# Experts' rows turned by a partition move and VectorE's block transpose in place of TensorE's transpose

## The chip, the cores and the metric

The kernel runs on one core of a Trainium2 chip. The metric is device time in microseconds (us) of one execution; lower is better. Engines: TensorE (PE; PEld is its weight load), VectorE (DVE), ScalarE (ACT), GpSimd (POOL), and SyncE (SP), which here only issues transfers. ACT and POOL have a queue for transfers too.

## The reference

Sliding-window attention (8 x 8 heads, 576 positions, head size 64, window 64) gives x, 4608 tokens of 512. A gate sends each token to one of 8 experts; a token keeps its predecessor's expert where a local gate is at least 0.5.

```python
logits = np.einsum('bsd,de->bse', x, w_gate)
local_gate = 1.0 / (1.0 + np.exp(-np.einsum('bsd,de->bse', x, w_local).squeeze(-1)))
...
            if s == 0 or local_gate[b, s] < 0.5:
                e = fresh_e
            else:
                e = prev_e if prev_e >= 0 else fresh_e
...
            h = np.maximum(x[b, s] @ w1[e], 0.0)
            out[b, s] = p[e] * (h @ w2[e])
```

w1 is 512 x 1024 and w2 1024 x 512 per expert, all in float32.

## The kernel before, in words

The attention comes first and writes its rows to the DRAM tensor `xs`; a router builds tables of row numbers, so that each *job* is a group of tokens of one expert: big (two tiles of 128 rows), small (one tile), half (64 rows) or quarter (32 rows). `Experts.run` writes out the order of the jobs by hand. Numbered from 0 it is: three big jobs from the first part of the tokens (0 to 2), then big 3, big 4, small 5, big 6, quarter 7, big 8, small 9, big 10, big 11, small 12, big 13, quarter 14, big 15, small 16, big 17, big 18, half 19, big 20, big 21, big 22, half 23.

For a job, `rows` lets POOL gather its rows from `xs` into a tile `xg` [128, 528], a token to a partition; `weights` lets SP load w1 and w2 (2 MB each) into a ring of four buffers. So the weights of job k+2 take the buffers that job k frees: w1 when its first product is done, w2 near the end of its second. Both are asked for at the start of iteration k, for job k+2.

`turn` puts features on partitions: four TensorE transposes per tile into PSUM (`tp`, L1196) and a copy to `xt` (L1197, on DVE from job 4 on). An iteration of a big job k is: `hidden(k)`, seven products of Strassen's scheme of 16 matmuls each (`product`, L1268) with `keep` copies on ACT (L1274) that read PSUM tiles which a later product adds into; `turn(k+1)`; `result(k)`, seven products of 8 matmuls (L1318), whose outputs ACT (L1323, L1349) and DVE (L1327) scale, and POOL scatters (L1394). DVE makes the sums that Strassen's scheme needs of the inputs (`xs`), the weights (`ws`) and the hidden values (`hs`) (L1220, L1231). Small jobs take plain matmuls (L1414, L1455; ReLU on ACT at L1425 and on DVE at L1423), halves L1414 and L1442.

From job 2 on the order on PE, SP, DVE and ACT is as written in the code; each engine runs its instructions in that order. Transfers of SP and ACT count, in turn, on one of eight semaphores, DMAHW0 to DMAHW7, and a transfer is issued only when the one before it on the same semaphore has landed.

Of the kernel before, what the change touches and what calls it, by code (L numbers as in the profile page):

```python
# [8 lines left out]
F32 = mybir.dt.float32  # L9
I32 = mybir.dt.int32  # L10
U32 = mybir.dt.uint32
BF16 = mybir.dt.bfloat16
# [7 lines left out]
P = 128  # L20
# [62 lines left out]
@with_exitstack  # L83
def kernel(
    ctx: ExitStack,
    tc: tile.TileContext,
    q: bass.AP,
    k: bass.AP,
    v: bass.AP,
    kq: bass.AP,  # L90
    v3: bass.AP,
    v4: bass.AP,
    vt: bass.AP,
    vh: bass.AP,
    wg: bass.AP,
    wg2: bass.AP,
    w1: bass.AP,
    w2: bass.AP,
    out: bass.AP,
):  # L100
    nc = tc.nc
    const = ctx.enter_context(tc.tile_pool(name="const", bufs=1))
    dram = ctx.enter_context(tc.tile_pool(name="dram", bufs=1, space=DRAM))


    xs = dram.tile([N + 2, PITCH], F32, name="xs")
    lt = const.tile([P, C, E + 1], F32, name="lt")
    tabs = dict(idx=const.tile([P, NS], U32, name="idx"), ej=const.tile([1, NBLK + 1], I32, name="ej"),
                idxh=const.tile([P, E], U32, name="idxh"), idxq=const.tile([P, E], U32, name="idxq"),
                idx1=const.tile([P, FIRST], U32, name="idx1"), ej1=const.tile([1, FB], I32, name="ej1"),  # L110
                gx=const.tile([P, NS], U32, name="gx"), gx1=const.tile([P, FIRST], U32, name="gx1"))
    ident = const.tile([P, P], F32, name="ident")
    make_identity(nc, ident)
    wg2s = const.tile([P, HP, GW], F32, name="wg2s")
    nc.gpsimd.dma_start(out=wg2s, in_=wg2)
    wgs = const.tile([P, DK, GW], F32, name="wgs")
    nc.gpsimd.dma_start(out=wgs, in_=wg)
    ok = const.tile([P, 1], F32, name="ok")
    bad, rare = const.tile([1, 1], I32, name="bad"), const.tile([1, 1], I32, name="rare")

    moe = xs, w1, w2, out, tabs, lt, ident
    with ExitStack() as fast:
        ring = fast.enter_context(tc.tile_pool(name="ring", bufs=4))
        rt = Router(fast, tc, lt, xs, tabs, ident)
        ex = Experts(fast, tc, ring, *moe)
        zeros, n = ex.xp.tile([P, PITCH], F32, name="xg"), (ZR - T1) // HF
        nc.vector.memset(zeros[:HF], 0.0)
        for i in (ZR, N + 1):
            nc.gpsimd.dma_start(out=xs[i:i + 1, :], in_=zeros[:1])
        nc.gpsimd.dma_start(out=xs[T1:ZR, D:].rearrange("(c p) o -> p c o", p=HF),  # L130
                            in_=zeros[:HF, :n * (PITCH - D)].rearrange("p (c o) -> p c o", c=n))
        attention(tc, ring, kq, v3, v4, vt, vh, xs, lt, ok, wgs, wg2s, ident, rt, ex)
        ex.run(fast, rt, lambda ps: flag(nc, ps, ok, bad, tabs["ej"][:, NBLK:], rare, ident))
    if_rare = nc.values_load(rare[0:1, 0:1], min_val=0, max_val=1,  # L134
                             skip_runtime_bounds_check_because="the larger of two comparisons")
    with tc.If(if_rare > 0):
        if_bad = nc.values_load(bad[0:1, 0:1], min_val=0, max_val=1,
                                skip_runtime_bounds_check_because="the result of a comparison")
        with tc.If(if_bad > 0):
            careful(tc, q, k, v, xs, lt, wgs, ident)  # L140
            with ExitStack() as slow:
                ring = slow.enter_context(tc.tile_pool(name="ring2", bufs=4))
                rt = Router(slow, tc, lt, xs, tabs, ident)
                rt.prepare()
                ex = Experts(slow, tc, ring, *moe)
                with tc.tile_pool(name="rt_ps1", bufs=1, space=PSUM) as ps:
                    for _ in rt.first(lambda: ps.tile([P, SC], F32, name="a")):
                        pass
                ex.begin()
                ex.run(slow, rt)  # L150
        if_more = nc.values_load(tabs["ej"][0:1, NBLK:], min_val=0, max_val=1,
                                 skip_runtime_bounds_check_because="the larger of two comparisons")
        with tc.If(if_more > 0), ExitStack() as slow:
            ring = slow.enter_context(tc.tile_pool(name="ring3", bufs=4))
            Experts(slow, tc, ring, *moe).more(slow)
# [12 lines left out]
def attention(ctx, tc, ring, kq, v3, v4, vt, vh, xs, lt, ok, wg, wg2, ident, rt, ex):  # L168
# [68 lines left out]
    def until(i, x):  # L237

        nc.sync.dma_start(out=late[:, i:i + 1], in_=x)
# [231 lines left out]
    for i, (sc, hp) in enumerate(units):  # L471
# [51 lines left out]
        if hp == 2 and sc + 2 in GATED:  # L523
            load(sc + 2, ["turned"])
        if (sc, hp) == (NSC - 3, 3):
            ex.jobs = [ex.weights({}, -1, ("w1",), lambda: until(2, allr[:1, sc, hp, 0, :1]))]
            if side == ():
                ex.rows(ex.jobs[0], -1)
        step(not (hp == 2 and sc + 1 in GATED))
# [601 lines left out]
class Experts:  # L1131
# [7 lines left out]

    def fetch(self, n):  # L1140

        return self.weights(self.rows({}, n), n)

    def rows(self, st, n):
        tabs = self.tabs
        if n < 0:
            idx, gx, rows = tabs["idx1"], tabs["gx1"], ZR + 1
            slots = range(-2 - 2 * n, -2 * n)
        else:
            idx, gx, rows = tabs["idx"], tabs["gx"], N + 2  # L1150
            slots = range(2 * n, 2 * n + 2) if n < NB else range(SM0 + n - NB, SM0 + n - NB + 1)
            if n >= KINDS[2]:
                slots = range(HF0 + n - KINDS[2], HF0 + n - KINDS[2] + 1)
        st.update(x=[], slots=slots, idx=idx, rows=P, big=len(slots) == 2, fast1=len(slots) == 2 and n not in PLAIN1,
                  fast2=len(slots) == 2 and n not in PLAIN2)
        if n >= KINDS[2]:
            st.update(quarter=n - KINDS[2], rows=QR)
        elif n >= KINDS[1]:
            st.update(half=n - KINDS[1], rows=HF)
        for s in slots:  # L1160
            x = (self.xp if n == -1 else self.xq).tile([P, PITCH], F32, name="xg")
            asked = self.nc.gpsimd.indirect_dma_start(  # L1162
                out=x, out_offset=None, in_=self.xs[:rows, :],
                in_offset=bass.IndirectOffsetOnAxis(ap=gx[:, s:s + 1], axis=0))
            st["x"].append(x)
            st["asked"] = asked
        st["pw"] = [x[:, D:D + 1] for x in st["x"]]
        return st

    def weights(self, st, n, names=("w1", "w2"), behind=lambda: None):  # L1170
        ej, at = (self.tabs["ej1"], -1 - n) if n < 0 else (self.tabs["ej"], n)
        e = self.nc.values_load(ej[0:1, at:at + 1], engines=[ET.SP], min_val=0, max_val=E - 1,
                                skip_runtime_bounds_check_because="a count of experts, at most E - 1")
        behind()
        for name, w, a, b in (("w1", self.w1, DK, F), ("w2", self.w2, FK, D)):
            if name not in names:
                continue
            t = self.ring.tile([P, a * b], F32, name="w")
            src = w[bass.ds(e, 1)].rearrange("o p x -> (o p) x")
            m = a * b // (PARTS if n < 0 else 1)  # L1180
            for c in range(0, a * b, m):
                self.nc.sync.dma_start(out=t[:, c:c + m], in_=src[:, c:c + m])
            st[name] = t.rearrange("p (a b) -> p a b", a=a)
        return st
# [4 lines left out]
    def turn(self, st, quiet, later=False):  # L1189
        nc, n = self.nc, st["rows"]  # L1190
        a = slice(HF, HF + n) if "quarter" in st else slice(n)
        st["xt"] = xt = self.xtp.tile([P, DK, BIG], F32, name="xt")
        for i, x in enumerate(st["x"]):
            tp = self.ps_t.tile([P, DK, P], F32, name="tp")
            for kk in range(DK):
                nc.tensor.transpose(tp[:, kk, :n], x[a, kk * P:(kk + 1) * P], self.ident[a, a])  # L1196
            (nc.scalar.copy if quiet else nc.vector.tensor_copy)(xt[:, :, i * P:i * P + n], tp[:, :, :n])  # L1197
# [276 lines left out]
    def run(self, ctx, rt, last=None):  # L1474
# [3 lines left out]
        ps_r = ctx.enter_context(tc.tile_pool(name="ex_ps_r", bufs=1, space=PSUM))  # L1478
        ctx.enter_context(tc.manual_schedule(engines={ET.PE, ET.SP}))
        rt.rows_of(ctx, tc, "rt_oh2", 3)  # L1480
        jobs = self.jobs

        def psum():
# [35 lines left out]
        for i, n in enumerate(order):  # L1519
            quiet = i < FB  # L1520
            if i == FB - 1:
# [2 lines left out]
                mark = last(self.ps_y.tile([P, D], F32, name="yp")) if last else None  # L1524

                ctx.enter_context(tc.manual_schedule(engines={ET.PE, ET.SP, ET.DVE, ET.Activation}))
                st = self.rows({}, order[FB])
                with tc.issue_after(st["asked"].ins):
                    jobs[i - 1].pop("later")()
                jobs.append(self.weights(st, order[FB]))  # L1530
                if jobs[i]["fast1"]:
                    self.prepare(jobs[i])
            if i + 2 > FB and i + 2 < len(order):
                jobs.append(self.fetch(order[i + 2]))
            if n >= KINDS[2]:
                continue
            if i == 1:
# [81 lines left out]
```

## Time and profile before

| | us |
|---|---|
| median of 3 runs | 644.74 (644.02 to 646.02) |
| the profiled execution | 642.1 |
| its span, first to last instruction | 640.0 |
| TensorE busy in the span | 615.6 |
| DVE, ACT, POOL busy | 402.3, 200.6, 133.1 |
| hardware DMA queue of SP | 135.54 MB, 58.4% of 16 engines' span |

The attention takes the first fifth of the span; the products of the experts' jobs follow up to 625. Busy times of a group are a union, so that matmuls that overlap in the pipeline count once. A row of the timeline gives start, duration, engine, line, operation, output and input, and how many instructions it merges. "DMA to landing" is the time from a transfer's issue to its landing.

### The profile page before, as it was taken

Reading aid. Unit: us, or ns where it says so; the run is one execution under the profiler, and the core shown is the slowest. Engines: PE = TensorE matmul, PEld = TensorE weight load, DVE = VectorE, ACT = ScalarE, POOL = GpSimd, SP = SyncE. Lnnn points to the kernel's source line nnn. Section 1 sums busy time; section 2 is a strip of 40 time slices with the busy share of each in tenths; the row PEclk is TensorE's granted clock in tenths of the full one; section 3 lists DMA queues with packets and bytes.
Section 4 is the critical chain, followed back from the end, with each engine's and each line's share of the span. In section 5 each row is a group of like instructions: output and inputs, shape, how many; then the busy total and the mean of one; then the engine's idle time right before and its main releaser. Section 6 shows DMA issues by size and latency. Waiting matters only on the chain. (4 is left out here: it accounts for less than half of the span.)

```text
span 640.0 us, 14994 instructions
## 1 busy us (share of the span) xinstructions
PE 615.6 (96%) x6367; PEld 544.2 (85%) x6367; DVE 402.3 (63%) x752; ACT 200.6 (31%) x368; POOL 133.1 (21%) x132
## 2 busy tenths in 40 slices
PE   8889998899999999999999999999999999999995
PEld 7777777788889999978997999887997998899994
DVE  6676588879968775273654683362917752886730
ACT  3766765612572122113120312021211221213120
POOL 5422112430103202120302120211312022111101
PEclk9999998999999999999999999999999999999998
DMA  9999996969757645786958665769768556956501
GB/s 338 416 418 406 385 366 241 348 236 337 237 171 246 244 166 198 242 316 236 387 189 291 218 234 212 259 235 367 263 228 324 185 199 232 379 167 225 209 17 38
DMA packets 29318, 166.43 MB, mean 260 GB/s; under 512 B 8451, under 2 KB 9497, under 8 KB 20026
## 3 DMA queue, kind: packets, MB, share of 16 engines
q1 hardware_dynamic: 20394, 135.54, 58.4%
q0 software_dynamic: 8848, 29.85, 12.2%
q8 instruction: 52, 0.85, 0.5%
q14 instruction: 24, 0.20, 0.1%
HBM read 146.18 MB, written 19.59 MB: 259 GB/s over the span
## 5 line engine op out<-in xcount | busy, mean ns | idle before, releaser
L1394 POOL DMA_INDIRECT out_dram<-y,idx x36 | 41.1, 1141 | 339.1 <-DVE y L1327 196.5
L1318 PE MATMUL hp<-ws,hs 128*128 128x256 f32 x384 | 88.7, 380 | 0.0
L1318 PEld LDWEIGHTS hp<-ws,hs 128*128 128x128 f32 x384 | 72.6, 190 | 10.5 <-issue 0.8
L1268 PE MATMUL hp<-xs,ws 128*128 128x128 f32 x672 | 79.6, 275 | 0.0
L1268 PEld LDWEIGHTS hp<-xs,ws 128*128 128x128 f32 x672 | 77.3, 192 | 0.0
L1327 DVE SCALAR_TENSOR_TENSOR y<-hp,xg,kept 128x256 f32<-128x256 f32 x48 | 22.6, 482 | 74.2 <-issue 47.0
L1414 PE MATMUL hp<-xt,w 128*64 128x64 f32 (+2 forms) x640 | 66.2, 276 | 0.0
L1414 PEld LDWEIGHTS hp<-xt,w 128*128 128x128 f32 (+1 forms) x640 | 60.8, 170 | 4.1 <-issue 0.7
L1318 PE MATMUL hp<-w,h 128*128 128x256 f32 x256 | 61.1, 382 | 0.0
L1162 POOL DMA_INDIRECT xg<-xs,gx x40 | 50.3, 1258 | 45.6 <-issue 37.4
L1279 DVE TENSOR_TENSOR h<-hp,keep 128x512 f32<-128x512 f32 x42 | 28.6, 690 | 48.1 <-PE hp L1268 48.0
L1268 PEld LDWEIGHTS hp<-xt,w 128*128 128x128 f32 x448 | 53.2, 192 | 2.7 <-issue 1.3
L1268 PE MATMUL hp<-xt,w 128*128 128x128 f32 x448 | 54.7, 275 | 0.0
L1318 PEld LDWEIGHTS hp<-w,h 128*128 128x128 f32 x256 | 47.2, 190 | 6.3 <-issue 0.4
L431 PE MATMUL xo<-vb,p 128*64 128x74 f32 (+1 forms) x576 | 44.5, 230 | 7.0 <-issue 2.9
L416 ACT ACTIVATE p<-sp 128x512 f32<-128x512 f32 x72 | 39.2, 595 | 38.0 <-PE sp L385 35.9
L385 PEld LDWEIGHTS sp<-w 64*64 64x64 f32 x1296 | 38.7, 138 | 12.1 <-issue 8.5
L421 DVE TENSOR_TENSOR p<-p,mask 128x1024 f32<-128x1024 f32 x29 | 36.1, 1245 | 19.5 <-ACT p L416 19.3
L431 PEld LDWEIGHTS xo<-vb,p 128*64 128x64 f32 x576 | 38.9, 138 | 9.9 <-issue 4.4
L385 PE MATMUL sp<-w 64*64 64x128 f32 (+1 forms) x1296 | 43.8, 270 | 2.6 <-issue 1.5
L431 PE MATMUL xo<-va,p 128*64 128x74 f32 (+1 forms) x576 | 44.5, 230 | 1.2 <-issue 1.2
L1280 ACT ACTIVATE h<-h 128x512 f32<-128x512 f32 x42 | 26.3, 630 | 59.1 <-DVE h L1279 59.1
(280 smaller groups left out, 955.0 us busy)
## 6 DMA issues: line engine op xcount, KB each, us to landing
w<-in_w_dram SPq DMA_DIRECT2D x42, 2048.0 KB, 9.2
w<-in_kq_dram SPq DMA_DIRECT2D x17, 1024.0 KB, 8.7
w<-in_w_dram SPq DMA_DIRECT2D x24, 512.0 KB, 9.3
xs<-x POOLq DMA_DIRECT2D x9, 1024.0 KB, 9.5
va<-in_v_dram SPq DMA_DIRECT2D x5, 1184.0 KB, 8.9
vtt<-in_vt_dram SPq DMA_DIRECT2D x5, 1024.0 KB, 7.2
va<-in_v_dram SPq DMA_DIRECT2D x3, 1040.0 KB, 12.2
va<-in_v_dram SPq DMA_DIRECT2D x2, 520.0 KB, 6.8
```

Source lines behind the costliest of these rows:

```text
L385: nc.tensor.matmul(sp[j][c * WIN:(c + 1) * WIN, a:b], lhsT=kt[h, hp, block * WIN:(block + 1) * WIN], rhs=qt[h, hp, a:b], start=not biased, ...
L416: nc.scalar.activation(p[:, j], sp[j], Act.Exp, scale=DH ** -0.5)
L421: masked.append(nc.vector.tensor_tensor(p, p, m.to_broadcast([P, 2, SC]), op=Alu.mult))
L431: nc.tensor.matmul(xo[par * WIN:(par + 1) * WIN, j, s * VW:s * VW + n], lhsT=p[:, j, b * WIN:(b + 1) * WIN], rhs=w[:, s, 2 * hp + j, :n], ...
L1162: asked = self.nc.gpsimd.indirect_dma_start(out=x, out_offset=None, in_=self.xs[:rows, :], in_offset=bass.IndirectOffsetOnAxis(ap=gx[:, s: ...
L1268: nc.tensor.matmul(out[:, m, :], lhsT=a[:, kk, m * P:(m + 1) * P], rhs=b[:, kk, :], start=start and m + kk == 0, stop=stop and (m, kk) == ...
L1279: nc.vector.tensor_tensor(o, x, y, op=add)
L1280: nc.scalar.activation(o, x if y is None else o, Act.Relu)
L1318: nc.tensor.matmul(out, lhsT=a[:, m, :], rhs=b[:, m, :], start=start and m == 0, stop=stop and m == FK // 2 - 1, skip_group_check=True)
L1327: nc.vector.scalar_tensor_tensor(y[i][:, j * w:(j + 1) * w], x, pw[i], y2, Alu.mult, Alu.add)
L1394: self.nc.gpsimd.indirect_dma_start(out=self.out[:, :], out_offset=bass.IndirectOffsetOnAxis(ap=st["idx"][:, s:s + 1], axis=0), in_=y, in_ ...
L1414: nc.tensor.matmul(hp[a, i, :], lhsT=st["w1"][:, kk, m * P:(m + 1) * P][:, a], rhs=st["xt"][:, kk, :n], start=(kk == 0), stop=(kk == DK - 1))
```

## The change

For the jobs of whole tiles from job 4 on (12 big, 4 small) TensorE's transposes and the copy from PSUM go. In their place `spread` (new) lets ACT issue four transfers per tile, each moving 128 features of 128 tokens from `xg` to a group of 32 partitions of a tile `rowh`: token 4t+m lands on partition t of the group, in slot m, in pieces of 512 bytes. `turn` then has DVE transpose blocks of 32x32 of that tile straight into `xt`. Features so lie on other partitions than before, and the load takes w1 from a host array `w1t` with its rows in the matching order. `rowh` tiles come from a pool of three that the router used for its tables.

```diff
@@ Experts.rows
+        st["plain"] = plain or n < 0 or st["rows"] < P
@@ Experts, new
+    def spread(self, st):
+
+        if st["plain"]:
+            return
+        st["sh"] = []
+        for x in st["x"]:
+            sh = self.shp.tile([P, PIECE, P], BF16, name="rowh")[:, :2 * DK].rearrange("p m t -> p (m t)")
+            sh = sh.bitcast(F32).rearrange("p (m t) -> p m t", m=4)
+            for a in range(4):
+                self.nc.scalar.dma_start(out=sh[a * QR:(a + 1) * QR].rearrange("t m d -> t (m d)"),
+                                         in_=x[:, a * P:(a + 1) * P])
+            st["sh"].append(sh)
@@ Experts.weights
-        for name, w, a, b in (("w1", self.w1, DK, F), ("w2", self.w2, FK, D)):
+        for name, w, a, b in (("w1", self.w1[not st["plain"]], DK, F), ("w2", self.w2, FK, D)):
@@ Experts.turn
         for i, x in enumerate(st["x"]):
+            if not st["plain"]:
+                nc.vector.transpose(xt[:, :, i * P:(i + 1) * P].rearrange("p j (t m) -> p m j t", m=4),
+                                    st["sh"][i].rearrange("p m (j d) -> p m j d", j=DK))
+                continue
             tp = self.ps_t.tile([P, DK, P], F32, name="tp")
@@ Experts.run
+        self.shp = rt.oh_p
...
+            if i >= FB and i + 1 < len(order) and not jobs[i + 1]["shared"]:
+                self.spread(jobs[i + 1])
             if i + 2 > FB and i + 2 < len(order):
-                jobs.append(self.fetch(order[i + 2]))
+                st = self.rows({}, order[i + 2])
+                st["shared"] = order[i + 1] >= KINDS[2]
+                if st["shared"]:
+                    self.spread(st)
+                jobs.append(self.weights(st, order[i + 2]))
@@ kernel (host)
+        "w1t": i["moe_w1"].reshape(E, 4, DK, QR, F).transpose(0, 1, 3, 2, 4).reshape(E, P, DK * F),
```

So the moves for job k+1 are issued at the start of iteration k. Where job k+1 is a quarter, it has none, and those of job k+2 are issued there instead.

On ACT, at the end of job 2's `result` and the start of job 3's `hidden`, with what each row waits for, there stood before:

```order
153 L1323 ACTIVATE kept_3167<-hp,xg 128x256 [waits PE_49]
154 L1349 ACTIVATE y<-hp,xg 128x256 [waits DMASW1_49,PE_49,Activation_49]
155 L1274 COPY keep_3221<-hp 128x512 [waits PE_49,Activation_49]
156 L1274 COPY keep_3231<-hp 128x512 [waits PE_49,Activation_49]
157 L1274 COPY keep_3241<-hp 128x512 [waits PE_49,Activation_49]
```

and stands now (names are the tiles'; DMASW is POOL's gather):

```order
154 L1368 ACTIVATE y<-hp,xg 128x256 [waits DMASW1_49,PE_49,Activation_49]
155 L1181 DMA rowh<-xg 32x4x128 [waits DMAHW1_49,DMASW2_49]
156 L1181 DMA rowh<-xg 32x4x128 [waits DMAHW2_49]
157 L1181 DMA rowh<-xg 32x4x128 [waits DMAHW3_49]
158 L1181 DMA rowh<-xg 32x4x128 [waits DMAHW4_49]
159 L1181 DMA rowh<-xg 32x4x128 [waits DMAHW5_49,DMASW3_49]
160 L1181 DMA rowh<-xg 32x4x128 [waits DMAHW6_49]
161 L1181 DMA rowh<-xg 32x4x128 [waits DMAHW7_49]
162 L1181 DMA rowh<-xg 32x4x128 [waits DMAHW0_49]
163 L1293 COPY keep_3231<-hp 128x512 [waits PE_49,Activation_49]
164 L1293 COPY keep_3241<-hp 128x512 [waits PE_49,Activation_49]
```

Eight moves for job 4 have come in ahead of the `keep` copies of job 3, each with its own semaphore in turn. The counts in the built program say which transfer stood before each on its semaphore: for the last two, on DMAHW7 and DMAHW0, these are the loads of w1 and w2 of job 4. On SP these two loads, and the next two (of job 5), stand as:

```order
104 L1197 DMA w<-in_w1t_dram 128x4096 [waits DMAHW7_49,DVE_49,PE_49]
105 L1197 ISA
106 L1197 DMA w<-in_w_dram 128x4096 [waits DMAHW0_49,DMAHW1_49,DVE_49,PE_49]
107 L1187 TENSOR_LOAD ej
108 L1197 ISA
109 L1197 DMA w<-in_w1t_dram 128x4096 [waits DMAHW1_49,DMAHW5_49,DVE_49,PE_49]
110 L1197 ISA
111 L1197 DMA w<-in_w_dram 128x4096 [waits DMAHW2_49,DMAHW6_49,DVE_49,PE_49]
```

They take the semaphores DMAHW7, 0, 1 and 2 in turn; what they wait for on PE and DVE is the release of their buffer. On PE, between `hidden` and `result` of job 3, the row `tp` is gone from the first to the second of these:

```order
989 L1268 MATMUL hp<-xs,ws_3141 128x128 x8
990 L1268 MATMUL hp<-xt,ws_3141 128x128 x8
991 L1268 MATMUL hp<-xs,w 128x128 x8
992 L1196 MATMUL tp<-ident,xg 128x128 x8
993 L1318 MATMUL hp<-w,h 128x256 x4
```

```order
988 L1287 MATMUL hp<-xt,w 128x128 x8
989 L1287 MATMUL hp<-xs,ws_3141 128x128 x8
990 L1287 MATMUL hp<-xt,ws_3141 128x128 x8
991 L1287 MATMUL hp<-xs,w 128x128 x8
992 L1337 MATMUL hp<-w,h 128x256 x4
```

On DVE the copies to `xt` are replaced in their places by the block transposes.

More of the change, by code (lines that the diff above doesn't have):

```diff
@@ L97 @@
     w1: bass.AP,
+    w1t: bass.AP,
     w2: bass.AP,
@@ L119 @@
     bad, rare = const.tile([1, 1], I32, name="bad"), const.tile([1, 1], I32, name="rare")
-    moe = xs, w1, w2, out, tabs, lt, ident
+    moe = xs, (w1, w1t), w2, out, tabs, lt, ident
     with ExitStack() as fast:
@@ L525, in attention @@
         if (sc, hp) == (NSC - 3, 3):
-            ex.jobs = [ex.weights({}, -1, ("w1",), lambda: until(2, allr[:1, sc, hp, 0, :1]))]
+            ex.jobs = [ex.weights({"plain": True}, -1, ("w1",), lambda: until(2, allr[:1, sc, hp, 0, :1]))]
             if side == ():
@@ L1140, in fetch, with rows @@
     def fetch(self, n):
-        return self.weights(self.rows({}, n), n)
-    def rows(self, st, n):
+        return self.weights(self.rows({}, n, True), n)
+    def rows(self, st, n, plain=False):
         tabs = self.tabs
@@ L1526, in run @@
                 ctx.enter_context(tc.manual_schedule(engines={ET.PE, ET.SP, ET.DVE, ET.Activation}))
-                st = self.rows({}, order[FB])
+                st = self.rows({}, order[FB], True)
                 with tc.issue_after(st["asked"].ins):
```

## Prediction

> **What bounds the kernel now.** I read the engines' busy shares first, then the stretches of the expert part, then TensorE's order of time in one iteration, and last the queues that feed it.
>
> ```profile
> PE 615.6 (96%) x6367; PEld 544.2 (85%) x6367; DVE 402.3 (63%) x752; ACT 200.6 (31%) x368; POOL 133.1 (21%) x132
> 300.00:640.00 340.00, 332.18 (x2555) 298.04 (x2553) 188.86 (x264) 69.11 (x126) 60.52 (x51) 0.99 0.64 232
> ```
>
> The second row gives PE, PEld, DVE, ACT and POOL busy, the granted clock, the DMA share and GB/s. TensorE is busy for 332 of the last 340 us at a clock of 0.99; DVE 189, ACT 69. So the end moves with whatever TensorE is given, and with whatever makes it wait. One iteration (job 2's second product, the start of job 3; start, duration):
>
> ```profile
> 203.98 1.04 PE L1196 MATMUL tp<-ident,xg 128*128 128x128 f32 x8
> 204.85 1.89 PE L1318 MATMUL hp<-w,h 128*128 128x256 f32 x8
> ...
> 215.21 1.89 PE L1318 MATMUL hp<-ws,h 128*128 128x256 f32 x8
> 216.94 1.95 PE L1268 MATMUL hp<-xt,w 128*128 128x128 f32 x16
> 218.72 3.74 PE L1268 MATMUL hp<-xs,ws 128*128 128x128 f32 x32
> 222.30 1.95 PE L1268 MATMUL hp<-xt,w 128*128 128x128 f32 x16
> 217.19 0.47 ACT L1349 ACTIVATE y<-hp,xg 128x256 f32<-128x256 f32 x1 [6.48 <-PE hp L1318]
> 218.98 0.59 ACT L1274 COPY keep<-hp 128x512 f32<-128x512 f32 x1 [1.32 <-PE hp L1268]
> 215.41 0.33 SPq L1182 DMA_DIRECT2D w<-in_w_dram  x1
> w<-in_w_dram SPq DMA_DIRECT2D x42, 2048.0 KB, 9.2
> ```
>
> Call the start of a job's first product T (here 216.94). The 32 matmuls at 218.72 are products 2 and 3, so product 3 starts at 218.72 + 3.58/2 = T+3.57. It adds into the PSUM tile that the first `keep` copy reads, and must wait for that copy; today the copy ends at 219.57, one microsecond early. At T-1.53 SP issues the second weight of the next job; such a load lands 9.2 us after its issue, so at T+7.7.
>
> **What is removed.** 24 tiles of 12 big jobs and 4 of small ones lose four transposes each, 112 in all. The eight of a big job hold TensorE from 203.98 to 204.85, 0.87 us; the four of a small one from 326.02 to 326.46, 0.44 us:
>
> ```profile
> 326.02 0.60 PE L1196 MATMUL tp<-ident,xg 128*128 128x128 f32 x4
> 326.46 1.89 PE L1318 MATMUL hp<-w,h 128*128 128x256 f32 x8
> ```
>
> 12 x 0.87 + 4 x 0.44 = 12.2 us, all of it on the bound. That is the whole gain.
>
> **What is moved to VectorE.** A PSUM copy becomes a block transpose of the same 128x512.
>
> ```profile
> 504.78 1.28 DVE L1197 COPY xt<-tp 128x512 f32<-128x512 f32 x2
> 506.10 0.42 DVE L1231 TENSOR_TENSOR xs<-xt 128x256 f32<-128x256 f32 x1
> ...
> 507.57 1.22 DVE L1220 TENSOR_TENSOR ws<-w 128x1024 f32<-128x1024 f32 x1
> 370.00:395.00 25.00, 25.00 (x173) 23.55 (x173) 17.03 (x23) 6.14 (x11) 4.66 (x4) 1.00 0.57 203
> ```
>
> Two copies take 1.28 us. No transpose stands in the trace; I bound a pair between 1.28 and, for a write with a stride of four elements at a quarter of the rate, 5.1 us, and take 1.28. The difference is hidden in DVE's 8 idle us of 25 (370 to 395), except at the half job below. The Trainium skill (VectorE: DVE Perf Modes, The three transpose paths) gives 311 ns for a 128x128 bf16 transpose; worked out from that, an estimate, a pair of 128x512 would be 8 x 0.311 = 2.5 us, and the sum below 1.2 us more. No run here shows it yet.
>
> **What is added, and where it waits.** 112 moves of 64 KB stand on ACT, eight (or four) together, between the last activation of one job and the first `keep` copy of the next. ACT runs in order. Each move also waits for the transfer before it on its semaphore, and SP's loads share the eight semaphores. I followed the counts through the built program: in 11 of the 12 groups of eight, the last one or two moves wait for the second weight of the job whose rows they move (or, with a quarter between, of the quarter), and that load was only issued around T. In the twelfth they wait for a first weight. Groups of four wait for older moves alone: ACT is free at T+0.72 (217.19 + 0.47), four issues of 0.33 end at T+2.0, the copy at T+2.6, in time.
>
> So behind the last move stand the `keep` copies, and behind the first of these product 3. What is late next is TensorE itself. After the landing come one issue (0.33, SP's row), the copy (0.59) and two handovers of 0.09 (a product ends at 218.89, its copy starts at 218.98): 1.1 us.
>
> First kind, a big job after a big one (T = 216.94 and 574.75, 2 times): landing T+7.7, copy done T+8.8, minus 3.57: 5.3 us each, 10.6.
>
> Second kind, a big job after a small one (4 times, the first at T = 282.32). A small job frees its second weight only at its end:
>
> ```profile
> 282.32 1.95 PE L1268 MATMUL hp<-xt,w 128*128 128x128 f32 x16
> 282.52 0.33 SPq L1182 DMA_DIRECT2D w<-in_w_dram  x1
> DMA to landing us min/median/max: 9.1/9.1/9.1
> ```
>
> Issue T+0.2, landing T+9.4 with the median: 9.4 + 1.1 - 3.57 = 6.9 us each, 27.7.
>
> Third kind, during a small job (4 times, the last at T = 475.05). ACT's first work there is a ReLU of 0.60 us that the second product needs:
>
> ```profile
> 473.52 0.33 SPq L1182 DMA_DIRECT2D w<-in_w_dram  x1
> 475.05 7.31 PE L1414 MATMUL hp<-xt,w 128*128 128x128 f32 x64
> 478.82 0.60 ACT L1425 ACTIVATE h<-hp 128x512 f32<-128x512 f32 x1 [3.05 <-PE hp L1414]
> 482.19 1.04 PE L1196 MATMUL tp<-ident,xg 128*128 128x128 f32 x8
> ```
>
> Landing T+7.7, ReLU done T+8.8; TensorE wants it at 482.19, T+7.14: 1.6 us each, 6.4.
>
> The half job (T = 540.67) and the big one behind it:
>
> ```profile
> 540.67 3.95 PE L1414 MATMUL hp<-xt,w 128*64 128x64 f32 x128
> 544.56 1.09 PE L1196 MATMUL tp<-ident,xg 128*128 128x128 f32 x8
> 545.58 3.67 PE L1442 MATMUL yp<-w,h 128*64 128x256 f32 x32
> 549.18 2.05 PE L1268 MATMUL hp<-xt,w 128*128 128x128 f32 x16
> 539.05 0.33 SPq L1182 DMA_DIRECT2D w<-in_w_dram  x1
> DMA to landing us min/median/max: 9.0/10.1/11.2
> w<-in_kq_dram SPq DMA_DIRECT2D x2, 512.0 KB, 3.9
> ```
>
> Its own products take 3.89 + 3.60 = 7.5 us and need nothing from ACT. But moves 7 and 8 go out only after the load of 539.05 lands (9.0, T+7.4), so at T+8.0. A move's flight isn't in the trace: more than its 64 KB at 367 GB/s (0.2 us), less than the 3.9 us of a 512 KB load; taking that load's 1.4 us of bytes off leaves 2.5, so 2.7. Landed T+10.8, transposed T+12.0: 4.5 us late; then product 2 waits for 1.47 us of `xs` and a first `ws` (1.25), against 1.78 of product 1: 0.9 more. 5.4 in all. The Trainium skill (DMA: Bandwidth & Descriptors, Anatomy of one DMA) puts the fixed cost of a DMA on GpSimd's path at about 2.0 us; if ACT's were the same, this would be 4.9. The job behind it (now at 552.7) waits in its group for a first weight issued at 544.67, landed at 555.9 by the 11.2 above; four issues, copy and handovers follow: 1.7 us.
>
> Waits: 10.6 + 27.7 + 6.4 + 5.4 + 1.7 = 51.8 us.
>
> **The clock.** An idle TensorE loses its clock here. Columns as above; the third value from the end is the granted clock:
>
> ```profile
> 98.00:100.00 2.00, 1.67 (x54) 1.37 (x50) 1.84 (x9) 1.98 (x3) 0.55 (x1) 1.00 0.98 366
> 101.00:102.00 1.00, 0.00 (x0) 0.00 (x0) 1.00 (x5) 0.90 (x2) 0.00 (x0) 1.00 0.40 150
> 102.00:103.00 1.00, 0.82 (x20) 0.82 (x22) 1.00 (x5) 0.00 (x0) 0.57 (x1) 0.82 0.22 73
> 104.00:105.00 1.00, 1.00 (x24) 1.00 (x26) 0.97 (x5) 0.00 (x0) 0.00 (x0) 0.50 0.98 403
> 106.00:107.00 1.00, 1.00 (x32) 1.00 (x32) 0.00 (x0) 0.95 (x2) 0.00 (x0) 0.98 0.40 139
> ```
>
> TensorE works the first 1.67 us from 98 and the last 0.82 before 103, so it idles from 99.67 to 102.18. After these 2.5 us the clock falls to 0.82, then 0.50 for three, then 0.98: 0.18 + 1.5 + 0.02 = 1.7 us lost. Seven waits are over 4 us: 11.9. The shorter ones I leave free; their upper end is 1.7 each.
>
> **Contention.** The first moves of a group fly beside the load that the last one waits for:
>
> ```profile
> 218.00:220.00 2.00, 2.00 (x20) 2.00 (x20) 1.97 (x3) 0.59 (x1) 1.70 (x2) 1.00 0.97 369
> ```
>
> The DMA engines are full there (0.97). Seven moves are 0.46 MB, at 369 GB/s 1.25 us; at least 0, if they only take gaps. I take half: 0.6 x 11 = 6.6.
>
> **Sum.** -12.2 + 51.8 + 11.9 + 6.6 = +58.1. The profiled execution took 642.1 us, so 700.2. It lies 2.6 below the median of the runs, 644.74: on that scale 702.8, and I say 702.
>
> **Rivals.** *Waits without their company*: neither clock nor contention adds. +51.8 - 12.2 = 39.6, 684. For it: the one clock fall in the trace follows one idle stretch only. Against it: these stalls are twice as long.
>
> *Crowding*: the 512-byte pieces cost the engines more than their bytes. With contention of 3 us per group in place of 0.6, +58.1 + 26 = 84, 729. For it: no transfer of such pieces between SBUF partitions stands in the trace. Against it: 56 pieces per engine and group would have to take 54 ns each.
>
> *Faster*: the load has landed, or the moves pass, before ACT needs it. Then the groups of eight end at T+0.72 + 8 x 0.33 = T+3.4, the copy at T+4.1, 0.5 us late in seven jobs: -12.2 + 3.5, 636. It decides from landings under T+2.5, 4.0 us after issue for the first kind. Against it: the 42 loads land in 9.2. For it: only that I have the waits from the program and not from a trace.
>
> *Slow transposes*: 5.1 us a pair adds 3.8 at the half job; in big jobs it stays within DVE's 8 us plus the new stalls. 707, inside the range.
>
> **Chances.** Full sum 0.68, waits alone 0.17, crowding 0.10, faster 0.04, no change 0.01. The range 676 to 724 goes from somewhat under the waits alone (landings of 8.7 in place of 9.2 take 5 us) to the sum with full contention (+7.2), the clock also at the four small jobs (+6.8) and slow transposes (+3.8), 721, and a little of crowding. Under 0.3%, about 2 us, no measurement here tells a change: faster 0.04, same 0.01, slower 0.95.
>
> **What would show it.** Right: ACT's row of `keep` copies ends idle time on DMA of `w`; TensorE waits on ACT `keep` by 5 to 7 us in six big jobs, on ACT `h` in four small ones; clock 0.5 behind these; TensorE's busy time about 12 us lower; DVE transposes waiting on nothing but in the half job. Wrong: `keep` copies at T+4 would refute the shared semaphores; moves landing later than 5 us would mean crowding; a pair of transposes over 8 us would make DVE the bound.

## The result, and the profile after

The change made the kernel slower: 718.81 us (median of 4 runs, 716.67 to 721.34) against 644.38 (643.69 to 646.02) for the kernel before beside it, a ratio of 1.115 (95% interval 1.110 to 1.119). Forecast were 702 us, with a range of 676 to 724. Ratios, here and below, leave out executions that took over 1.5% longer than the fastest of the same kernel.

The page of the kernel after (span, busy times, TensorE's granted clock in 40 slices):

```profile
span 718.8 us, 14992 instructions
...
PE 627.3 (87%) x6255; PEld 550.9 (77%) x6255; DVE 413.0 (57%) x752; ACT 199.9 (28%) x368; POOL 126.3 (18%) x132
...
PEclk9999999999999999799997998789997999798998
```

The profiled execution took 720.53 us. The span grew by 78.8 us. TensorE's idle time grew from 640.0 - 615.6 = 24.4 to 718.8 - 627.3 = 91.5, by 67.1; its busy time grew by 11.7 with 112 instructions fewer, and the clock row has nine slices under 9, where before it had two.

Who ended TensorE's and ACT's idle time (waiting engine, tile and line, then the releaser; us in total, times, longest):

```profile
PE hp L1287 <- ACT keep L1293: 37.2, 7, 8.3
PE hp L1287 <- issue: 14.4, 2, 9.9
PE yp L1474 <- ACT h L1444: 9.1, 4, 3.9
PE hp L1337 <- DVE y L1346: 5.4, 6, 1.0
```

```profile
ACT keep L1293 <- DMA rowh<-xg: 54.1, 6, 10.5
...
ACT h L1444 <- DMA rowh<-xg: 24.8, 3, 9.8
ACT y L1464 <- DMA rowh<-xg: 10.7, 1, 10.7
```

These four rows of TensorE make 66.1 us, against the 67.1 by which its idle time grew ("issue" is 9.88 at the end of the half job and 4.55 in job 21, the latter behind a `keep` too). Behind them ACT waits for the moves, as foreseen: on `keep` in big jobs, on the ReLU `h` in small ones. One stall of each main kind, from the timelines of ACT, SP and TensorE, with the last of the eight moves in a row of its own (start, duration; a queue's row, "ACTq" or "SPq", goes from the first issue to the end of the last). Job 3, T = 216.74, a big job after a big one:

```profile
215.21 0.33 SPq L1197 DMA_DIRECT2D w<-in_w_dram  x1
217.07 5.26 ACTq L1181 DMA_DIRECT2D rowh<-xg  x7
224.37 0.55 ACTq L1181 DMA_DIRECT2D rowh<-xg  x1
225.02 1.07 ACT L1293 COPY keep<-hp 128x512 f32<-128x512 f32 x2 [7.56 <-DMA rowh<-xg]
225.66 3.65 PE L1287 MATMUL hp<-xs,ws 128*128 128x128 f32 x16 [5.18 <-ACT keep L1293]
```

Job 6, T = 291.18, a big job after a small one:

```profile
291.37 0.33 SPq L1197 DMA_DIRECT2D w<-in_w_dram  x1
291.44 5.32 ACTq L1181 DMA_DIRECT2D rowh<-xg  x7
301.65 0.55 ACTq L1181 DMA_DIRECT2D rowh<-xg  x1
302.25 1.07 ACT L1293 COPY keep<-hp 128x512 f32<-128x512 f32 x2 [10.18 <-DMA rowh<-xg]
302.88 3.78 PE L1287 MATMUL hp<-xs,ws 128*128 128x128 f32 x16 [7.97 <-ACT keep L1293]
```

In both jobs seven moves go out without a long wait and the eighth stands still: for 2.04 us in job 3, for 4.89 in job 6. It goes out 0.02 us after the last part of the load that stands before it on its semaphore has landed (at 224.35 and 301.63 by the trace's landing times). So the wait that the prediction named is there. But the seven issues alone take 5.3 us: without the eighth move's wait, by subtraction, some 3.1 us of job 3's 5.18 and of job 6's 7.97 would be left.

Job 21, T = 645.58, is the other big job after a big one:

```profile
642.83 0.33 SPq L1197 DMA_DIRECT2D w<-in_w_dram  x1
645.93 7.20 ACTq L1181 DMA_DIRECT2D rowh<-xg  x8
653.86 3.78 PE L1287 MATMUL hp<-xs,ws 128*128 128x128 f32 x16 [4.55 <-issue]
```

Here the load lands at 652.43, before ACT's seventh issue ends (652.47). No move waits for it, and the eight issues, 0.85 us each on average, make the whole stall. The half job, its rows of ACT, VectorE and TensorE:

```profile
598.63 10.59 ACTq L1181 DMA_DIRECT2D rowh<-xg  x8
616.21 1.99 DVE L1210 STREAM_TRANSPOSE xt<-rowh 128x512 f32<-128x512 f32 x2 [11.69 <-DMA rowh<-xg]
617.39 3.75 PE L1287 MATMUL hp<-xt,w 128*128 128x128 f32 x16 [9.88 <-issue]
```

The prices of the two new operations stand in the rows of the tile `rowh` (durations in ns: min/median/max, first and last start):

```profile
L1181 ACTq DMA_DIRECT2D rowh<-xg x112: 554/644/1937, 217.1 to 652.5; - x112
...
L1210 DVE STREAM_TRANSPOSE xt<-rowh x28: 1057/1093/1112, 238.7 to 668.8; 128x512 f32<-128x512 f32 x28
```

A move takes 0.64 us of ACT's queue, twice SP's 0.33. A block transpose takes 1.09 us where the copy took 0.68.

### The profile page after: what moved, and what is told of

It reads as the page before. It is cut to its first block, busy times and chain, and to the rows that moved or that the text cites. A ratio compares the mean times of both kernels' runs of the same rounds, so it can differ in the third digit from the quotient of the medians.

```text
span 718.8 us, 14992 instructions
## 1 busy us (share of the span) xinstructions
PE 627.3 (87%) x6255; PEld 550.9 (77%) x6255; DVE 413.0 (57%) x752; ACT 199.9 (28%) x368; POOL 126.3 (18%) x132
## 3 DMA queue, kind: packets, MB, share of 16 engines
q10 hardware_dynamic: 16128, 7.35, 4.8%
## 5 line engine op out<-in xcount | busy, mean ns | idle before, releaser
L1287 PE MATMUL hp<-xs,ws 128*128 128x128 f32 x672 | 92.6, 298 | 42.1 <-ACT keep L1293 37.2
L1287 PEld LDWEIGHTS hp<-xs,ws 128*128 128x128 f32 x672 | 87.8, 212 | 44.2 <-ACT keep L1293 38.5
L1287 PEld LDWEIGHTS hp<-xt,w 128*128 128x128 f32 x448 | 59.1, 210 | 12.6 <-issue 12.2
L1287 PE MATMUL hp<-xt,w 128*128 128x128 f32 x448 | 60.1, 292 | 9.9 <-issue 9.9
L1164 POOL DMA_INDIRECT xg<-xs,gx x40 | 46.6, 1164 | 69.9 <-issue 61.9
L1293 ACT COPY keep<-hp 128x512 f32<-128x512 f32 x42 | 23.9, 587 | 118.1 <-PE hp L1287 56.9
L422 DVE TENSOR_TENSOR p<-p,mask 128x1024 f32<-128x1024 f32 x29 | 37.0, 1278 | 19.2 <-ACT p L417 19.1
```

The costliest lines, as they stand in the source:

```text
L422: masked.append(nc.vector.tensor_tensor(p, p, m.to_broadcast([P, 2, SC]), op=Alu.mult))
L1164: asked = self.nc.gpsimd.indirect_dma_start(out=x, out_offset=None, in_=self.xs[:rows, :], in_offset=bass.IndirectOffsetOnAxis(ap=gx[:, s: ...
L1287: nc.tensor.matmul(out[:, m, :], lhsT=a[:, kk, m * P:(m + 1) * P], rhs=b[:, kk, :], start=start and m + kk == 0, stop=stop and (m, kk) == ...
L1293: nc.scalar.copy(o, x)
```

## Experiments

Three theories stood: (1) the two moves that share a semaphore with a fresh weight load hold ACT, and the clock falls behind the stalls; (2) the issues on ACT take the time, or the 512-byte pieces crowd the DMA engines; (3) VectorE's slower turn makes the loss. Below, "the interval of a job" is the time from the start of its first product to that of the next job, read from TensorE's timeline.

### Only the two moves elsewhere

```diff
+    def move(self, n):
+        for o, x in self.moves[:n]:
+            self.nc.scalar.dma_start(out=o, in_=x)
+        del self.moves[:n]
@@ spread
-                self.nc.scalar.dma_start(out=sh[a * QR:(a + 1) * QR].rearrange("t m d -> t (m d)"),
-                                         in_=x[:, a * P:(a + 1) * P])
+                self.moves.append((sh[a * QR:(a + 1) * QR].rearrange("t m d -> t (m d)"), x[:, a * P:(a + 1) * P]))
@@ run, behind each spread
+                self.move(6)
@@ big_hidden (and in hidden behind ACT's ReLU; in run ahead of turn)
         relu(hq[1][1], px, z)
+        self.move(8)
```

> The same 112 moves on ScalarE's queue, same bytes, but of each group of eight only the first six stay where they were; the last two, which share a semaphore with the fresh weight load, are issued behind the second sum's ReLU of a big job (behind the ReLU of a small one). My theory (these two wait for the load and hold the copies behind them): the six issues at 0.64 us end at T+4.6, the first keep copy at T+5.2, 1.6 us late in six jobs in place of 4.6 to 8.3; the small jobs' stalls vanish; the half job's 10 us stay. 718.8 - 49.6 + 9.6 - about 19 of clock = 660 us (650 to 668). Rival, the issues themselves take the time (eight took 7.85 us): three quarters of the stalls stay, about 700. Rival, the 512-byte pieces crowd the DMA engines: about 715, for the pieces are all there.

Measured: 667.88 us (660.66 to 671.04), a ratio of 1.033 (1.026 to 1.040). Job 3 (T = 219.53), ACT and TensorE:

```profile
219.86 4.12 ACTq L1174 DMA_DIRECT2D rowh<-xg  x6
224.71 2.05 PE L1291 MATMUL hp<-xs,ws 128*128 128x128 f32 x16 [1.45 <-ACT keep L1297]
```

And a row of TensorE's waits:

```profile
PE hp L1291 <- ACT keep L1297: 9.1, 7, 2.7
```

Six issues take 4.12 us, and TensorE waits 1.45 us; with the two more they took 7.85, and it waited 5.18. In all 9.1 us on `keep` stay, as expected (9.6), where issue time alone would have left three quarters of some 50. So two moves of eight make most of the loss, with all bytes still moved. That is not all the wait for the load, though: this edit also takes two issues of eight from ahead of the copy. The trace after the change parts the two. In the ten stalls of big and small jobs behind a group of eight (49.6 us), the eighth move's wait for the load makes 29.0, and the issues the other 20.6.

The profiled execution here, 671.04 us, has a span of 669.3, 9.5 more than my figure of 659.8, which starts from a span. The clock falls that I took as gone were not all gone: two remain behind the half job and in job 21, 3.8 us, and two others in the attention go with a start of job 3 that is 2.8 us later. TensorE waits another 2.7 us on VectorE's `ws`. The half job (18.9 us) keeps its stall, as I had reckoned.

### The moves on GpSimd's queue

```diff
-                self.nc.scalar.dma_start(out=sh[a * QR:(a + 1) * QR].rearrange("t m d -> t (m d)"),
+                self.nc.gpsimd.dma_start(out=sh[a * QR:(a + 1) * QR].rearrange("t m d -> t (m d)"),
```

> The same moves issued on GpSimd's queue, whose transfers have semaphores of their own, so that none waits for a weight load and none stands ahead of a copy on ScalarE. My theory (the wait on the load, on ScalarE): the stalls on keep and h vanish, what stays is the half job (about 5 of waiting and 3 of clock) and VectorE's slower block transposes (5.4): 642 - 12 + 13 = 643, with 637 to 655. Rival, crowding by the pieces: over 690. Rival, issue time on ScalarE: 643 too; the run with six and two tells that one.

Measured: 640.32 us (638.72 to 643.57), a ratio of 0.994 (0.992 to 0.996). The busy times of its page:

```profile
PE 607.3 (95%) x6255; PEld 534.2 (83%) x6255; DVE 413.2 (65%) x752; ACT 200.5 (31%) x368; POOL 186.2 (29%) x244
```

The largest row of TensorE's waits from 200 us on:

```profile
PE hp L1337 <- DVE y L1346: 4.7, 5, 1.0
```

No wait on ACT is left, nor the half job's stall, which I had kept in my sum: GpSimd also comes to its moves sooner, and those of the job behind the half job are out by 523.6, 13 us before the half job starts. The same 112 moves in the same pieces cost TensorE nothing by crowding. The same 6255 matmuls are busy for 607.3 us here and 627.3 after the change: of these 20.0 us the clock's falls make 19.1 (below).

### The moves without their use

```diff
@@ weights
-        for name, w, a, b in (("w1", self.w1[not st["plain"]], DK, F), ("w2", self.w2, FK, D)):
+        for name, w, a, b in (("w1", self.w1[0], DK, F), ("w2", self.w2, FK, D)):
@@ turn
-            if not st["plain"]:
+            if False:
```

> TensorE's transposes and the plain weights stay, and the moves are issued on ScalarE at the places of the change, but nothing reads what they moved. My theory: the stalls on keep and h stay with their clock loss (49.6 + about 19), the half job and VectorE's part (9.9 + 5 + 5.4) go, and the 12.2 of transposes come back: 718.8 + 12.2 - 20.3 = 711 (700 to 718). Rival, the block transpose on VectorE makes the loss: 645 to 655.

Measured: 724.0 us (718.54 to 728.22), a ratio of 1.126 (1.121 to 1.131). The largest row of TensorE's waits:

```profile
PE hp L1287 <- ACT keep L1293: 46.0, 8, 8.9
```

The moves alone make the whole loss; VectorE has its old copies back. My number was missed by 13 us. I had taken the half job's stall out, and its interval did shrink (10.2 us in place of 19.0), but the job behind it grew from 28.2 to 36.4: the stall had moved, not gone.

### The turn without the moves

```diff
@@ turn
-                                    st["sh"][i].rearrange("p m (j d) -> p m j d", j=DK))
+                                    x[:, :4 * P].rearrange("p (m j d) -> p m j d", m=4, j=DK))
@@ run: both calls of spread are left out
```

> No moves: VectorE turns the gathered rows as they lie, so that features and tokens are mixed up and the result of these 16 jobs is another one; the move between partitions is left out. It is the price of the turn alone. My theory: 642 - 12.2 + 5.4 (VectorE's later outputs of the second layer, seen in the changed kernel) = 635, on the median's scale 637 to 639. Rival, the slow block transpose makes the loss: over 650.

Measured: 639.2 us (636.76 to 643.15), a ratio of 0.992 (0.990 to 0.994): VectorE's turn doesn't make the loss. But it gains little too. From the first product of job 3 to that of job 23 the kernel before takes 408.6 us, this one 405.1: 3.5 us of the 12.2. The four small jobs and the two pairs of a big job and a quarter fall by the full 0.87 to 0.88, jobs 4 and 11 by 0.43; but jobs 3, 10, 17 and 21 rise from 25.47 to 25.86, the half job and the one behind it by 0.5 each, and jobs 8 and 15 stay. VectorE and TensorE at the end of job 3:

```profile
232.28 2.02 DVE L1210 STREAM_TRANSPOSE xt<-xg 128x512 f32<-128x512 f32 x2
...
239.40 1.22 DVE L1239 TENSOR_TENSOR ws<-w,ws 128x1024 f32<-128x1024 f32 x1
240.54 1.26 DVE L1346 SCALAR_TENSOR_TENSOR y<-hp,xg,kept 128x256 f32<-128x256 f32 x3
241.46 1.99 PE L1337 MATMUL hp<-ws,h 128*128 128x256 f32 x8 [1.00 <-DVE y L1346]
```

The outputs `y` stand behind the turn and eight sums without a gap, and the last product waits for them. TensorE comes 0.87 us sooner, VectorE 0.74 us later (2.02 for a pair in place of 1.28).

### The moves spread out on ScalarE

```diff
@@ as with the two moves, but ahead of the first keep
-                self.move(6)
+                self.move(2 if jobs[i]["fast1"] else 4)
@@ big_hidden
         u = keep(0, px)
+        self.move(2)
...
         z = keep(1, py)
+        self.move(2)
@@ run, where job i + 1 is the half job
-                st = self.rows({}, order[i + 2])
+                st = self.rows({}, order[i + 2], order[i + 1] >= KINDS[1] and order[i + 1] < KINDS[2])
```

> All moves on ScalarE's queue as in the change, but put where ScalarE is free: of each eight, two ahead of the first keep copy, two behind it, two behind the second, two behind the second sum's ReLU (in a small job four ahead of its ReLU, four behind); the job behind the half job keeps TensorE's transposes. My theory (only what stands behind the two moves that wait for a load is late): no stall on keep or h, what stays is VectorE's later outputs, so as with GpSimd's queue, 637 to 645. Rival, issuing on ScalarE is itself too dear (eight issues of 0.64 are 5 us of each 25): 650 to 670. Rival, crowding: over 690, but GpSimd's queue has already spoken against it.

Measured: 646.36 us (644.02 to 650.0), a ratio of 1.004 (1.002 to 1.006). No wait of TensorE on `keep` or `h` is left. The issues still take ACT 72 us in all (104 moves; the job behind the half job has none). So it is their place that takes away the loss: issues and waits now lie where nothing is due behind them. It is still 6 us above GpSimd's queue. VectorE's transposes now wait for the moves, and the outputs with them (a row of VectorE's waits, one of TensorE's, and the moves' landing times):

```profile
DVE xt L1214 <- DMA rowh<-xg: 15.6, 5, 4.4
```

```profile
PE hp L1344 <- DVE y L1353: 6.5, 5, 2.0
```

```profile
DMA to landing us min/median/max: 2.2/8.2/13.7
```

### The half job without moves

```diff
-                st = self.rows({}, order[i + 2])
+                st = self.rows({}, order[i + 2], order[i + 1] >= KINDS[1] and order[i + 1] < KINDS[2])
```

> The change, but the big job behind the half job keeps TensorE's eight transposes and the plain weights, so that the half job carries no moves. It is the price of the half job's term with its clock: that job took 19.0 us in the changed kernel and 8.5 before, the next one 28.2 against 25.6. My theory: 718.8 - 10.5 - 2.6 = 706 (702 to 709). Rival, the stall only goes to the next wait: 715 to 719.

Measured: 718.51 us (717.77 to 719.23), no gain: the rival was right. The half job takes its old 8.5 us, but the job behind it 37.8 in place of 28.2. SP, ACT and TensorE there:

```profile
600.46 0.34 SPq L1197 DMA_DIRECT2D w<-in_w1t_dram  x1
605.15 4.18 ACTq L1181 DMA_DIRECT2D rowh<-xg  x6
611.47 5.71 ACTq L1181 DMA_DIRECT2D rowh<-xg  x2
617.28 1.07 ACT L1293 COPY keep<-hp 128x512 f32<-128x512 f32 x2 [11.72 <-DMA rowh<-xg]
617.92 3.78 PE L1287 MATMUL hp<-xs,ws 128*128 128x128 f32 x16 [9.11 <-ACT keep L1293]
```

The same load and the same moves, of job 21, after the change:

```profile
604.08 0.34 SPq L1197 DMA_DIRECT2D w<-in_w1t_dram  x1
613.00 7.58 ACTq L1181 DMA_DIRECT2D rowh<-xg  x8
```

In both built programs one of these eight moves (the seventh here, the fifth there) stands behind that load of job 21's first weight. After the change the half job's stall lets the moves come 8.9 us after the load's issue; without it they come 4.7 us after, and their issues take 12.0 us in place of 7.6. The load is only a part of that: by the semaphores in the trace the seventh move waits 2.1 us for it, and the eighth 4.6 us for the first move of its own group, which was issued at 605.15 and landed at 616.61.

### A version that beats both

With the moves on GpSimd's queue, VectorE's outputs could go ahead of two weight sums that only the fifth and sixth product need:

```diff
@@ prepare makes sums 1 and 2 of the weights; 3 and 4 are kept back
+        def rest():
+            put(s3, a[0][0], a[1][0], op=Alu.subtract)
+            put(s4, a[0][1], s2, op=Alu.subtract)
+        self.rest.append(rest)
@@ big_result (and big_hidden, ahead of prepare2)
         put(0, 1, py, v)
+        self.finish()
@@ run, in the half job (not in the last version)
+            if "half" in jobs[i]:
+                self.early(jobs[i + 1])
             self.turn(jobs[i + 1], i + 1 < FB)
```

> GpSimd's queue for the moves, and on VectorE the last two of the four weight sums of a big job are put behind the three outputs of the job before it (they are needed only by its fifth and sixth product); at the half job the first two sums go ahead of the block transposes. My theory (turn alone gained 3.5 of 12.2 us because each pair of transposes makes the last output late, 1.25 us in five jobs with a big one behind, and about 2 at the half job): 640.3 - 6.3 - 1 = 633 (631 to 636). Rival, VectorE is simply full and the sums are late elsewhere: 638 to 644.

Measured: 638.67 us with a wide spread, 632.56 to 642.76, a ratio of 0.991 (0.987 to 0.995). Jobs 3, 10 and 17 take 24.6 us, as hoped, but the profiled execution (642.76) has one new stall, in job 20. GpSimd, VectorE and TensorE:

```profile
553.23 1.01 POOL L1483 DMA_INDIRECT out_dram<-y,idxh  x1 [9.86 <-ACT h L1316]
554.23 3.86 POOL L1181 DMA_DIRECT2D rowh<-xg  x7
562.56 0.55 POOL L1181 DMA_DIRECT2D rowh<-xg  x1 [4.47 <-DMA out_dram<-y,idxh]
564.32 1.08 DVE L1210 STREAM_TRANSPOSE xt<-rowh 128x512 f32<-128x512 f32 x1 [8.16 <-DMA rowh<-xg]
570.30 3.78 PE L1354 MATMUL hp<-ws,h 128*128 128x256 f32 x8 [7.06 <-DVE y L1363]
```

Seven moves stand behind the half job's scatter in GpSimd's order, and the eighth shares a semaphore with that scatter and waits for it to land: the same kind of wait as in the change, on the other queue.

> The kernel before with the same two reorderings of VectorE's sums and nothing else. My theory: there the outputs are in time by 0.06 us already, so nothing is gained: 643 to 646. Rival, what the run with GpSimd's queue gains comes from the reordering alone: 636 to 640.

Measured: 643.84 us (641.59 to 644.71), a ratio of 1.000 (0.998 to 1.001). The kernel before has nothing from the reordering.

Two versions without that stall followed. In the first, job 21 keeps TensorE's transposes:

```diff
-                st = self.rows({}, order[i + 2])
+                st = self.rows({}, order[i + 2], i > FB and KINDS[1] <= order[i] < KINDS[2])
```

> The run with GpSimd's queue and the later sums, but the second big job behind the half job (order position 21) keeps TensorE's transposes. In that run its last move stood behind the half job's scatter on GpSimd and landed late, which made the job ahead of it 33.7 us long in place of 25.2. My theory (a move that waits for another transfer, here a scatter, is again all that is left): 641.0 - 8.5 + 0 = 632.5 by the profiled execution, 631 to 635 as a median, and less spread than 632.6 to 642.8. Rival, the loss goes to another job's moves: 637 to 641.

Measured: 634.08 us (633.04 to 634.48) against 641.67 (640.88 to 644.77) beside it, a ratio of 0.987 (0.984 to 0.991). The busy times of its page, and the largest row of TensorE's waits from 200 us on:

```profile
PE 605.2 (96%) x6263; PEld 533.2 (84%) x6263; DVE 412.3 (65%) x752; ACT 200.8 (32%) x368; POOL 190.5 (30%) x236
```

```profile
PE hp L1354 <- DVE y L1363: 0.6, 1, 0.6
```

In the second, the sums of the half job stay where they were, and with them GpSimd's order of the run without reordering:

> GpSimd's queue and the last two weight sums behind the three outputs, for big jobs only; the half job's sums stay where they were, and with them GpSimd's order of the run without reordering (four moves ahead of the half job's scatter, four behind). My theory: each big job ahead of a big one takes 24.6 in place of 25.86 us, four times, and the job behind the half job stays at 26 us: 640.3 - 5 = 635 (633 to 638). Rival, the job behind the half job is long here too: 639 to 643.

Measured: 634.7 us (632.8 to 635.85), a ratio of 0.988 (0.984 to 0.991). It moves all 112 and keeps no job on TensorE's transposes. Between first products (of job 3 and of the last half job) the two take 399.2 and 399.0 us, 9.4 and 9.5 less than the kernel before.

## Why the prediction was right, and where its sizes were off

The path is shown, not only argued: moves on ACT, then `keep` or ReLU, then TensorE. Taking two moves of eight out of ACT's way takes most of the loss away, other places on the same engine nearly all of it, another queue all of it, and the moves alone, unused, make all of it. What held ACT was told only in part. The sum let the load's landing set the end of every group and took 0.33 us for an issue. The wait for the load is there: in nine of the twelve groups of eight the eighth move goes out when that load lands. But the issues, 0.70 us each on average, make 20.6 of the 49.6 us of stalls, and without any load they alone would have left a stall of about 3 us or more in each of the six big jobs. That the forecast of 5.3 us came near the 4.55 of job 21, where no move waited for a load, is luck: there the issues happened to end when the load landed. The term by term account, in us:

| term of the sum | predicted | measured | |
|---|---|---|---|
| transposes removed | -12.2 | -3.5 | the turn alone, late outputs included |
| first kind, 2 stalls | 10.6 | 9.7 | 5.18 and 4.55 |
| second kind, 4 | 27.7 | 30.8 | 7.97, 8.34, 7.12, 7.35 |
| third kind, 4 | 6.4 | 9.1 | the row of `yp` |
| half job | 5.4 | 9.9 | |
| job behind it | 1.7 | 0 | |
| groups of four | 0 | 1.2 | 0.99 and 0.21 |
| clock | 11.9 | 19.1 | see below |
| contention | 6.6 | none of its own | GpSimd's queue has none |

The forecast was 17 us short of the median. The misses in the table, which is taken from one execution, are 7.2 (clock), 8.7 (the gain), 4.5 (half job), 5.8 (second and third kind) and 1.2, less 6.6, 1.7 and 0.9: 18.2.

**The clock.** The step that failed took one fall of 1.7 us for each of seven long waits, from an idle stretch of 2.5 us. Stretches of 1 us around two stalls (TensorE's busy share leads; the third value from the end is the granted clock):

```profile
225.00:226.00 1.00, 0.34 (x2) 0.34 (x3) 0.00 (x0) 0.98 (x2) 0.84 (x1) 0.92 1.18 211
226.00:227.00 1.00, 1.00 (x7) 1.00 (x7) 0.00 (x0) 0.09 (x1) 0.00 (x0) 0.50 1.24 225
...
229.00:230.00 1.00, 1.00 (x10) 1.00 (x10) 0.00 (x0) 0.58 (x1) 0.00 (x0) 0.88 0.00 0
...
299.00:300.00 1.00, 0.00 (x0) 0.00 (x0) 0.85 (x1) 0.00 (x0) 0.00 (x0) 0.50 1.00 233
...
307.00:308.00 1.00, 1.00 (x8) 1.00 (x8) 0.00 (x0) 0.29 (x1) 0.00 (x0) 0.62 0.00 0
```

Behind the 5.18 us of job 3 the fall is what I took, 1.65 us of lost clock. Behind 8 us the clock is at 0.50 before TensorE starts again at 302.88, and stays there until 307.6: 2.4. Summed over all such stretches from 205 on (busy time times the missing share of the clock), eight falls lose 19.1 us: one of 1.65 and seven of 2.2 to 2.7. The eighth is in a small job, behind a wait of 3.90 us of the kind that I had left free, and a wait of 4.55 us cost 2.7: the length of the wait doesn't set the price.

The trace's clock record shows what does. The eight falls begin at 225.83, 297.51, 379.43, 444.29, 461.35, 543.27, 611.54 and 652.50, always a whole number of 3.413 us apart, and last 3.42 us (once), 6.83 (twice) or 10.24 (five times): one, two or three steps of the same grid. A step in which TensorE idled for more than 2.1 us of its 3.41 was followed by one at half the clock; the step from 219.01, with 1.95 us idle at the start of job 3's stall, was not. Once fallen, the clock came back after a step with at most 0.25 us idle and stayed low after one with 0.72 or more. This fits all twelve traces from 30 us to the end of the matmuls: no step with less than 1.75 us idle was followed by a fall, every one with more than 1.95 was, and in between both occur. A fall costs half of what TensorE works in these steps. So it matters where a wait lies on the grid: the 4.55 us from 649.31 fill most of one step and reach 1.36 us into the next, which keeps the clock low for a second step, and cost more than the 5.18 us of job 3.

**The half job.** The step that failed is the flight of a move, 2.7 us. The seventh move does wait for the load, until 606.07 (T+7.7, as told), but this isn't what TensorE waited for. The first transpose, at 616.21, needs only the first tile's four moves, all out by 601.65; the fourth of them landed at 616.09, 15.2 us after its issue. Even the eighth waits, until 608.67, for the first move of its own group, 10.0 us in flight. The moves fly beside 2 MB loads; on ACT's queue in the spread-out version the median is 8.2 and the least 2.2. The Trainium skill (DMA: Bandwidth & Descriptors, Anatomy of one DMA) gives about 2.0 us of fixed cost for a transfer of GpSimd's path; the least here, on ACT's queue, is near it. By the prediction's own sign (moves that land later than 5 us mean crowding) this would be crowding; it cost TensorE time here because the moves were needed at once.

**The gain of 12.2.** The step that failed is "the difference is hidden in DVE's 8 idle us of 25". Idle time elsewhere in an iteration is no cover for work ahead of outputs that are due: 0.74 us more per pair cost the gain wherever a big job follows a big one. I chose 1.28 us, the lower end, for a pair; it took 2.02. The Trainium skill (VectorE: DVE Perf Modes, The three transpose paths), from which I had 2.5 as an estimate, was nearer.

**Second and third kind.** The wait ends with the load, as told, and the loads land a little later: in job 6 the last move is out 10.8 us after the load's issue, where 9.2 and one issue of 0.33 were expected; the four loads of the second kind land 9.4 to 10.6 us after their issue. Contention does show there, if it is that, but as a part of these stalls and not beside them. An issue takes 0.64 us (the median) in place of 0.33, which the load's flight hides here, since the seven issues end before it lands.

**Job behind the half.** The step that failed took its group to wait for a load alone. After the change its first two moves wait for moves of the half job's group (the first goes out at 613.00, the second stands still for 2.33 us), but TensorE stalls as long, so nothing is left to wait for behind them. The two runs that freed the half job show the stall coming back there, and in the run without its moves 4.6 us of ACT's waits are for a move and 2.1 for the load.

**Two of the signs** did not come as written. TensorE's busy time was to fall by about 12 us and grew by 11.7: the prediction's own clock term of 11.9 would already have cancelled that sign. And the block transposes waited for moves in the four small jobs too (2.9 to 4.7 us), at no cost that shows on TensorE.

What stays open: why an issue on ACT takes between 0.55 and 1.94 us, and how far the later landings come from the moves' own bytes, was not measured alone.

## What to carry to other kernels

When a transfer is added to an engine that also computes, list what stands before it on its semaphore and what stands behind it in the engine's order: a 64 KB move that shares a semaphore with a 2 MB load costs the engine what is left of the load's flight, 1.4 to 5.0 us here, and each issue costs it 0.6 to 0.7 us besides. Take away a stall only together with its cause, since a stall can be what makes the next wait short. And before work on one engine is counted as free on another, look whether an output that the first one needs stands behind it: the gain came only once the sums that were not yet due had been put behind that output.

## What the runs showed of the hardware beyond expectation

Issuing a move of 128 partitions by 512 bytes took ACT's queue 0.55 to 1.94 us (median 0.64) and GpSimd 0.55, against 0.33 for a 2 MB load on SP. A fall of the clock cost 1.65 us behind a wait of 5.18 us, but 2.7 behind one of 4.55, 2.6 behind one of 3.90 and 2.2 to 2.7 behind those of 7 to 10; the waits of 1.4 to 2.1 us in the other small jobs cost none. In every trace, from 30 us on, the falls of the clock began on one grid of 3.413 us, each behind a step of it in which TensorE had idled for 1.75 us or more. A move of 64 KB was in flight for 2.2 to 16.0 us after the change, with a median of 8.7, beside loads of 2 MB with a median of 9.2. A block transpose of 128x512 in float32 took 1.09 us, against 0.68 for a copy of the same size from PSUM.
